# A fused attention and MLP kernel: fetching transposed activations for two tiles in one set of transfers

## The chip, the cores and the metric

The kernel runs on one core of a Trainium2 chip. A core has a matrix engine (TensorE, PE in the profile; its weight loads are shown as PEld), a vector engine (VectorE, DVE), a scalar engine (ScalarE, ACT), a general engine (GpSimd, POOL) and a sync engine (SyncE, SP), which here does nothing but issue DMA transfers. The metric is the device time of one execution in microseconds. Of the kernel before, three runs took 875.13, 876.93 and 880.14 us; the median is 876.93 us.

## The reference

```python
def _attn_ref(q, k, v, g_norm):                       # q, k, v: 8 x 8 x 576 x 64
    kv = np.einsum('bhsd,bhse->bhde', k, v)
    out = np.einsum('bhsd,bhde->bhse', q, kv)
    rms = np.sqrt(np.mean(out * out, axis=-1, keepdims=True) + 1e-06)
    return (out / rms * g_norm)

def _moe_ref(x, w_in, w_out):                         # x: 4608 x 512
    h = x @ w_in                                      # w_in: 512 x 2048
    r = np.maximum(h, 0.0)
    return (r * r) @ w_out                            # w_out: 2048 x 512
```

The attention has no softmax: every head's keys and values are multiplied to a 64 x 64 matrix, and the queries with that. Its output, normalized per token and head, is the `x` of the two matrix products behind it. The weights arrive as float64 and are converted in the opening part of the kernel; everything else is float32.

## The kernel before, in words

The 4608 tokens make 36 tiles of 128 tokens, numbered 0 to 35, and nine strips of four tiles, numbered 0 to 8. For each strip there is an up phase (`x @ w_in`, then relu and square) and a down phase (`@ w_out`). Both are computed with seven products in place of eight over 2 x 2 blocks, from strip 2 on at two levels, so that sums and differences of blocks are formed on DVE and POOL, and PE reads blocks of weights that were formed once, stored in DRAM (`w_deep`, `w_in_deep`, `w_out`) and are streamed back as `w_blk`, block by block, by `stream()`. In the trace a strip from strip 2 on takes PE some 90 us.

While PE works on a strip, the other engines prepare the next strip's `x` in small pieces put between the steps (`slices`, `attend_between`): products of queries and key-value matrices (`query`, line 468), squares and means, the root, the scaled result, and then the transpose, since PE needs `x` with features on partitions. For tiles 0 to 8 PE itself transposes (`features`). Tiles 9 to 35 take another way, in three steps:

- `squares_x(n)` (line 645): DVE transposes tile n within 32 x 32 squares;
- `send_x(n)` (line 654): one transfer of 256 KB stores it in a DRAM tile `x_d`, and an entry is put into the queue `tiles_due`;
- `fetch_x(n)` (line 661): four transfers of 64 KB, one per group of 32 features, read it back in the order that PE needs, into the strip's tile `xT`.

`open_xt(s)` takes the buffer of `xT` from `stream_pool`, the pool of six buffers that also holds the streamed blocks `w_blk`. It is called by the first `fetch_x` of a strip.

The order of all instructions on each engine is the order in which the Python code emits them. What decides when a fetch is emitted is a counted clock (`clock[0]`; from strip 2 on 1.2 units for a step of an up phase and 3.2 for a step of a down phase): an entry of `tiles_due` falls due 6 units after the send, or 24, 30 or 36 for tiles 11, 9 and 10. At each step the main loop emits at most one thing: a due load of keys and values (`keys_due`), or else a due fetch, or else, if enough clock has passed since the last one, one "drip": a pair of query transfers from `drips` (`load`, line 123, two transfers of 64 KB) or `rest_drips` (`load_q_rest`, line 176, two of 16 KB). At the eleventh step of a down phase all fetches that the next strip still lacks are emitted.

```python
elif not due(keys_due) and not (soon and due(tiles_due)):
    ...
    if not quiet and clock[0] >= dripped[0] + least:
        dripped[0] = clock[0]
        drip(True)
```

All these transfers go out on one queue, SP's, in program order, and an instruction that waits holds up everything behind it. In the built program each of SP's transfers waits, besides for its data and its buffer, for the landing of a transfer some eight before it on the queue, since eight semaphores are used in turn. The lines of the queue that matter below: 123 (queries), 132 and 162 (keys, values), 176 (the rest of the queries), 654 and 661 (`x_d`, `xT`), 939 (blocks of `w_in_deep`, for the up phase), 945 and 951 (blocks of `w_out` and `w_deep`, for the down phase), 960 (output). On DVE: line 384 transposes queries that have landed, line 1300 adds a product from PSUM to a unit of the hidden layer or a snapshot of it, lines 289 and 1046 form differences and sums. PE's products of both phases have line 842.

Of the kernel before, what the change touches and what calls it, by code (L numbers as in the profile page):

```python
# [10 lines left out]
FP32 = mybir.dt.float32  # L11
# [9 lines left out]
def kernel(  # L21
# [34 lines left out]
    nc = tc.nc  # L56
    P = 128
# [4 lines left out]
    NP = H // 2  # L62
# [6 lines left out]
    NT = 4  # L69
# [2 lines left out]
    N_STRIP = N_TILE // NT  # L72
    DEEP = 1
    DEEP_UP = 2
    SQ = 32
    Q_ON_PE = 2
    BEHIND = 1.6
# [10 lines left out]
    dram = ctx.enter_context(tc.tile_pool(name="dram", bufs=1, space=bass.MemoryType.DRAM))  # L88
# [15 lines left out]
    def load(b, p, q_eng, names="kvq", parts=range(4)):  # L104
# [9 lines left out]
        for i, (n, src, eng) in enumerate(inputs if b == 0 else inputs[1:] + inputs[:1]):  # L114
# [3 lines left out]
            if n == "q" and b >= Q_ON_PE:  # L118

                t = qkv_pool.tile([P, 4 * C, SQ], FP32, name=n, tag=n, bufs=3) if 0 in parts else main[n, b, p]  # L120
                for a in parts:
                    h, f = divmod(a * SQ, D)
                    eng.dma_start(
                        out=t[ts(a, SQ)],
                        in_=src[b, 2 * p + h, 0 : C * P, f : f + SQ].rearrange("(k i) f -> i k f", k=4 * C),
                    )
# [28 lines left out]

    squares = lambda t: t.rearrange("p h d -> p (h d)").rearrange("p (k q f) -> p k q f", k=4, f=SQ)

# [6 lines left out]
    def load_q_rest(b, eng, one=None):  # L164
# [8 lines left out]
        for a in range(4) if one is None else (one,):  # L173
            hq, f = divmod(a * SQ, D)
            for kq in range(2):
# [14 lines left out]
    drips, rest_drips, keys_due, tiles_due = deque(), deque(), deque(), deque()  # L190
    clock, dripped = [0.0], [0.0]
# [382 lines left out]
    first = {}  # L574
# [49 lines left out]
    def open_xt(s):  # L624
        if s not in xt:
            if s == 0:
                xt[s] = xt_pool.tile([P, STRIP // SQ, NP, SQ], FP32, name="xT", tag="xT")
            else:
                t = stream_pool.tile([P, 4, FQ // 2, P], FP32, name="xT", tag="w_blk")
                xt[s] = t.rearrange("p n f e -> p (n f e)").rearrange("p (a q t) -> p a q t", q=NP, t=SQ)  # L630
        return xt[s]
# [18 lines left out]
    squared, sent = {}, {}  # L650

    def send_x(n):
        d = sent[n] = dram.tile([P, 4, NP, SQ], FP32, name="x_d", tag="x_d", bufs=2 * NT)
        nc.sync.dma_start(out=d, in_=squared.pop(n))
        tiles_due.append((clock[0] + {9: 30, 10: 36, 11: 24}.get(n, 6), fetch_x, (n,)))

    def fetch_x(n):
        s, i = divmod(n, NT)
        x, d = open_xt(s), sent.pop(n)
        for f in range(4):  # L660
            nc.sync.dma_start(
                out=x[ts(f, SQ), ts(i, 4)].rearrange("d a q t -> d a (q t)"),
                in_=d[:, f].rearrange("(a d) q t -> d a (q t)", a=4),
            )

    xc = {}
# [44 lines left out]
    for b in range(2, B):  # L711
        pairs = query_pairs(b)
        for i, pair in enumerate(pairs):
# [11 lines left out]
            if b == 2:  # L725
                slices += [(T, (3, 1))] * (left == 1) + [(mean_roots, (pair,)), (normalized, (pair,))]
                slices += [(T, (3, 0))] * (left == 2) + [(squares_x, (n,)) for n in pair]
                for n in pair:
                    slices.append((send_x, (n,)))
                    if n % NT == NT - 1:  # L730
                        ready[n // NT] = len(slices)
                pair_ends.append(len(slices))
                continue
# [4 lines left out]
            for t, n in enumerate(pair):  # L738
                slices += [(squares_x, (n,)), (send_x, (n,))]
                if n % NT == NT - 1:  # L740
                    ready[n // NT] = len(slices)
                if t == 0:
                    slices += heads[3:]
# [5 lines left out]
    def attend(n):  # L749
        while slice_at[0] < min(n, len(slices)):  # L750
            fn, a = slices[slice_at[0]]
            fn(*a)
            slice_at[0] += 1
# [171 lines left out]
    for s in range(DEEP, N_STRIP):  # L925
        to_stream += [("in", s, p) for p in UP_SETS if s >= DEEP_UP]
        to_stream += [(s, p, n) for p in DEEP_ORDER for n in range(2)]
# [181 lines left out]
    def down_deep(s, k, i):  # L1109
# [3 lines left out]
        if s == N_STRIP - 1 and k == 6 and i == 1:  # L1113
# [19 lines left out]
            return  # L1133
        if k == 0 and s >= DEEP_UP:
            if i == 0:
# [71 lines left out]
    def deep_differences_in(b):  # L1207
        minus(nc.gpsimd, w_half(b, 0, 1), w_half(b, 0, 0), w_half(b, 0, 1))
# [18 lines left out]
    def leaf_x(s, n):  # L1227

        x = operand_x(s, UP_SETS[n])
        t = leaf_t[s, n] = sum_pool.tile([P, 4, TH // SQ // 2, SQ], FP32, name="x_l", tag="sum")  # L1230
        late = x[:, 4:8].rearrange("p a k t -> p k a t")
        minus(nc.gpsimd, t[:, 0:2], late, x[:, :, 0].rearrange("p (h a) t -> p h a t", h=2))
        minus(nc.gpsimd, t[:, 2], late[:, 1], t[:, 0])
        minus(nc.gpsimd, t[:, 3], x[:, 0:4, 1], t[:, 2])
# [13 lines left out]
    def up_slot(s, slot):  # L1248
# [8 lines left out]
        if at == 0 and 0 < n < 6:  # L1257
            leaf_x(s, n + 1)
        if s == DEEP_UP and at == 0 and n < 7:
            deep_differences_in(A_IN[UP_SETS[n]])  # L1260
# [77 lines left out]
    for s in range(N_STRIP):  # L1338
        attend(ready[s])
        if s == DEEP_UP - 1:  # L1340
            while queried:
# [3 lines left out]
            apsum = ctx.enter_context(tc.tile_pool(name="apsum", bufs=1, space=bass.MemoryType.PSUM, reuse_waits="tile"))  # L1345
        if s >= DEEP_UP:
            steps = [(0.5, up_slot, (s, slot)) for slot in range(55)]
# [10 lines left out]
        goal, begun = ready.get(s + 1, len(slices)), slice_at[0]  # L1358
        if s >= DEEP_UP:
            goal = max(goal, min(ready[DEEP_UP] + (len(slices) - ready[DEEP_UP]) * (s - 1) // (N_STRIP - DEEP_UP - 1), len(slices)))  # L1360
# [3 lines left out]
        for i, (w, fn, a) in enumerate(steps):  # L1364
# [33 lines left out]
            if s:  # L1398
                clock[0] += 3.2 if i >= n_up else 2.2 if s == DEEP else 1.2
                soon = tiles_due and tiles_due[0][2][0] // NT == s + 1  # L1400
                if i == n_up + 10:
                    while tiles_due and tiles_due[0][2][0] // NT == s + 1:
                        _, f, a = tiles_due.popleft()
# [36 lines left out]
            n = i + 1 - (n_up - 6)  # L1440
# [44 lines left out]
```

## Time and profile before

| | us |
|---|---|
| median of three runs | 876.93 |
| time of the profiled execution | 876.18 |
| its span in the profile | 874.4 |
| PE busy in the span | 860.8 |
| DVE busy | 722.9 |
| ACT busy | 352.0 |
| POOL busy | 315.4 |
| DMA: mean rate over the span | 270 GB/s |

Among the DMA issues of the page, `xT<-x_d` stands with 108 transfers of 64 KB at a median of 4.1 us from issue to landing, and `x_d<-x_q` with 27 of 256 KB at 5.3 us. The granted TensorE clock is 1.00 in every stretch of the profile. All times of single instructions are counted from the start of the span. The profiled execution took 1.8 us more than its span; this part lies outside of what the profile shows.

How to read the views: the windows give the busy time of each engine in a stretch; 20.00 of 20.00 for PE means that it was never without a matmul. The view of waits says for how long an engine stood idle and what ended it. The timeline lists instructions in order, with the start, the duration, and in brackets the idle time of the engine before it; for SP, the duration is that of issuing, and the transfer lands later.

### The profile page before, as it was taken

The numbers are of one execution on the slowest core, as the hardware profiler recorded it, in microseconds if no ns is written. First come the engines' busy times: TensorE is split into PE (matmuls) and PEld (weight loads), VectorE is DVE, ScalarE is ACT, GpSimd is POOL, SyncE is SP. The second block draws the span as 40 slices with busy tenths as digits, with TensorE's granted clock in tenths as the row PEclk, the third lists the DMA queues.
The fourth block names the chain that finished last, engine by engine and source line by source line (L and its number), as shares of the span: only waits on it lengthen the run. The fifth ranks groups of instructions, "written<-read, shape, count | busy, mean of one in ns | idle before, by whom it ended". The sixth has DMA issues, their size and how long they took to land.

```text
span 874.4 us, 32665 instructions
## 1 busy us (share of the span) xinstructions
PE 860.8 (98%) x14176; PEld 805.8 (92%) x14176; DVE 722.9 (83%) x1236; ACT 352.0 (40%) x805; POOL 315.4 (36%) x319
## 2 busy tenths in 40 slices
PE   8999999999999899999999999999999999999998
PEld 7445888889999899999999999999999999999998
DVE  3899998879867896889778977897889777975897
ACT  5799241320047402560358034811392147202710
POOL 1100004630458305650475045704471447144700
PEclk9999999999999999999999999999999999999999
DMA  9998998999988997989778978998668856885483
GB/s 306 328 311 251 285 372 237 283 339 346 305 219 205 338 328 242 239 290 338 245 213 261 344 268 228 271 346 287 189 238 293 295 173 218 299 283 196 175 313 120
DMA packets 170304, 236.49 MB, mean 270 GB/s; under 512 B 79536, under 2 KB 134576, under 8 KB 161840
## 3 DMA queue, kind: packets, MB, share of 16 engines
q1 hardware_dynamic: 169856, 234.33, 82.5%
q8 instruction: 111, 1.82, 0.8%
q14 instruction: 33, 0.27, 0.1%
q10 hardware_dynamic: 304, 0.07, 0.0%
HBM read 197.66 MB, written 36.70 MB: 268 GB/s over the span
## 4 chain that ended last, share of the span: by engine, by line
PE 82%; DVE 9%; DMA 4%; ACT 3%; issue 2%; SPq 1%; DVEq 0%; ACTq 0%
PE ps_A L842 35%; PE ps_B L842 30%; PE ps_C L842 5%; PE ps_A L847 4%; PE x_ps L468 2%; PE kv_ps L432 2%; PE ps_B L847 2%; DVE w_c L269 1%; DVE w_t L289 1%; DMA q<-in_q_dram 1%; DMA w_blk<-w_deep 1%; DMA w_deep<-w_t 1%; DVE wt L289 1%; DMA q_rest<-in_q_dram 1%; PE ps_C L847 1%
## 5 line engine op out<-in xcount | busy, mean ns | idle before, releaser
L842 PE MATMUL ps_B<-w_blk,g_s 128*64 128x128 f32 x2016 | 122.6, 273 | 0.0
L842 PEld LDWEIGHTS ps_B<-w_blk,g_s 128*64 128x64 f32 x2016 | 113.1, 137 | 0.1
L842 PE MATMUL ps_A<-x_l,w_in 128*64 128x128 f32 x1568 | 102.4, 273 | 0.6 <-ACT snap L1305 0.6
L289 POOL TENSOR_TENSOR x_l<-xT 128x256 f32<-128x256 f32 x21 | 15.9, 757 | 232.4 <-PE ps_A L842 184.3
L842 PE MATMUL ps_B<-w_blk,gt 128*64 128x128 f32 x1504 | 94.7, 273 | 2.8 <-DMA w_blk<-w_deep 1.6
L842 PE MATMUL ps_A<-w_blk,g_s 128*64 128x128 f32 x1536 | 92.7, 273 | 0.4 <-issue 0.4
L842 PEld LDWEIGHTS ps_A<-x_l,w_in 128*64 128x64 f32 x1568 | 88.9, 137 | 0.9 <-ACT snap L1305 0.8
L842 PEld LDWEIGHTS ps_B<-w_blk,gt 128*64 128x64 f32 x1504 | 85.1, 137 | 3.6 <-issue 2.2
L1300 POOL TENSOR_TENSOR snap<-snap,gt 128x512 f32<-128x512 f32 x35 | 46.2, 1319 | 113.1 <-ACT snap L1305 107.5
L842 PEld LDWEIGHTS ps_A<-w_blk,g_s 128*64 128x64 f32 x1536 | 86.1, 137 | 0.5 <-issue 0.5
L1305 ACT COPY snap<-ps_A 128x512 f32<-128x512 f32 x63 | 36.8, 585 | 105.0 <-PE ps_A L842 99.0
L1240 ACT ACTIVATE gt<-gt 128x512 f32<-128x512 f32 x112 | 70.1, 626 | 14.2 <-DVE gt L1300 14.2
L1241 ACT ACTIVATE gt<-gt 128x512 f32<-128x512 f32 x112 | 70.7, 631 | 3.6
L842 PE MATMUL ps_A<-w_blk,gt 128*64 128x128 f32 x1152 | 71.5, 273 | 0.0
L842 PEld LDWEIGHTS ps_A<-w_blk,gt 128*64 128x64 f32 x1152 | 65.0, 137 | 0.0
L1089 ACT COPY o_sb<-ps_A 128x128 f32<-128x128 f32 x24 | 6.4, 265 | 145.5 <-PE ps_A L842 110.2
L1088 DVE TENSOR_TENSOR o_sb<-o_sb,ps_B 128x256 f32<-128x256 f32 (+1 forms) x123 | 47.4, 386 | 15.8 <-ACT o_sb L1089 11.0
L289 DVE TENSOR_TENSOR gt<-gt 128x2048 f32<-128x2048 f32 (+1 forms) x29 | 59.7, 2063 | 0.0
L1300 POOL TENSOR_TENSOR gt<-gt,snap 128x512 f32<-128x512 f32 x42 | 52.6, 1282 | 17.7 <-DVE snap L1300 17.7
L842 PE MATMUL ps_B<-x_l,w_blk 128*64 128x128 f32 x784 | 51.3, 273 | 0.0
L842 PE MATMUL ps_A<-x_l,w_blk 128*64 128x128 f32 x784 | 51.2, 273 | 0.0
L1046 DVE TENSOR_TENSOR g_s<-gt 128x512 f32<-128x512 f32 x56 | 47.9, 856 | 0.0
(194 smaller groups left out, 1801.6 us busy)
## 6 DMA issues: line engine op xcount, KB each, us to landing
w_blk<-w_deep SPq DMA_DIRECT2D x56, 1024.0 KB, 7.2
w_blk<-w_out SPq DMA_DIRECT2D x56, 768.0 KB, 6.7
w_blk<-w_in_deep SPq DMA_DIRECT2D x49, 768.0 KB, 6.1
raw<-in_moe_w_in_dram SPq DMA_DIRECT2D x16, 512.0 KB, 7.0
raw<-in_moe_w_out_dram SPq DMA_DIRECT2D x16, 512.0 KB, 4.8
k<-in_k_dram SPq DMA_DIRECT2D x29, 256.0 KB, 4.8
v<-in_v_dram SPq DMA_DIRECT2D x29, 256.0 KB, 5.1
x_d<-x_q SPq DMA_DIRECT2D x27, 256.0 KB, 5.3
```

Of the source, the lines that this page charges most:

```text
L269: yield nc.vector.scalar_tensor_tensor(out=ci, in0=high, scalar=-(2**30), in1=ci, op0=ALU.bitwise_and, op1=ALU.bitwise_or)
L289: eng.tensor_tensor(out=out, in0=a, in1=b, op=ALU.subtract)
L432: nc.tensor.matmul(ps[ts(h, D), i], lhsT=a, rhs=w, start=i == 0 and c == 0, stop=c == C, skip_group_check=True)
L468: nc.tensor.matmul(ps[half, r, i, ts(p, D)], lhsT=q[row, half], rhs=kvd[b, p][row, row], start=True, stop=True)
L842: nc.tensor.matmul(ps[half], lhsT=lhsT[:, half], rhs=rhs, start=start, stop=stop, skip_group_check=True)
L847: nc.tensor.matmul(bank[BANK[p]][:, i, :], lhsT=lhsT(k), rhs=rhs(k), start=p in (1, 5, 2) and i == 0 and k == 0, stop=k == n - 1, skip_gro ...
L1046: nc.vector.tensor_tensor(out=t, in0=a21, in1=a22, op=ALU.add)
L1088: add = lambda out, a, b: nc.vector.tensor_tensor(out=out, in0=a, in1=b, op=ALU.add)
L1240: nc.scalar.activation(o, o, AF.Relu)
L1241: nc.scalar.activation(o, o, AF.Square)
L1300: add = lambda eng, out, a, b: eng.tensor_tensor(out=out, in0=a, in1=b, op=ALU.add)
L1305: nc.scalar.copy(t, ps)
```

## The change

`send_x` now gives two neighbouring tiles (an even number and the odd one behind it) one DRAM tile with two halves, and only the odd tile's send puts an entry into `tiles_due`. `fetch_x` then reads both halves with four transfers of 128 KB. Tile 8 is transposed on PE, so tile 9, the first that is sent, is fetched alone as before (`FIRST_SENT`). The even tile has no due time of its own any more; the entry for tile 10 is gone. There are 56 fetches in place of 108, with the same bytes.

```diff
+    FIRST_SENT = 9
...
     def send_x(n):
-        d = sent[n] = dram.tile([P, 4, NP, SQ], FP32, name="x_d", tag="x_d", bufs=2 * NT)
-        nc.sync.dma_start(out=d, in_=squared.pop(n))
-        tiles_due.append((clock[0] + {9: 30, 10: 36, 11: 24}.get(n, 6), fetch_x, (n,)))
-
-    def fetch_x(n):
+        if n % 2 and n - 1 in sent:
+            d = sent.pop(n - 1)
+        else:
+            d = dram.tile([2, P, 4, NP, SQ], FP32, name="x_d", tag="x_d", bufs=NT)
+        sent[n] = d
+        nc.sync.dma_start(out=d[n % 2], in_=squared.pop(n))
+        if n % 2:
+            tiles_due.append((clock[0] + {9: 30, 11: 24}.get(n, 6), fetch_x, (n, 1 if n == FIRST_SENT else 2)))
+
+    def fetch_x(n, tiles):
         s, i = divmod(n, NT)
         x, d = open_xt(s), sent.pop(n)
+        first = i + 1 - tiles
         for f in range(4):
             nc.sync.dma_start(
-                out=x[ts(f, SQ), ts(i, 4)].rearrange("d a q t -> d a (q t)"),
-                in_=d[:, f].rearrange("(a d) q t -> d a (q t)", a=4),
+                out=x[ts(f, SQ), 4 * first : 4 * (i + 1)].rearrange("d a q t -> d a (q t)"),
+                in_=d[2 - tiles :, :, f].rearrange("n (a d) q t -> d (n a) (q t)", a=4),
             )
```

## The prediction

> **What bounds the kernel now.** I read the page's first part, then the windows for where PE is idle, then PE's waits, and then, for the one stretch that stands out, the chain and the timelines of SP, PE and DVE.
>
> ```profile
> PE 860.8 (98%) x14176; PEld 805.8 (92%) x14176; DVE 722.9 (83%) x1236; ACT 352.0 (40%) x805; POOL 315.4 (36%) x319
> ```
>
> PE is busy for 98% of the span. A change that leaves PE's instructions alone can only win from the 874.4 - 860.8 = 13.6 us that are left. The windows, from the first stretch in which the new program differs (about 211 us):
>
> ```profile
> 200.00:240.00 40.00, 40.00 (x738) 40.00 (x736) 36.60 (x55) 2.17 (x7) 9.73 (x10) 1.00 0.98 322
> 240.00:260.00 20.00, 19.74 (x420) 19.30 (x416) 14.88 (x29) 8.98 (x28) 10.66 (x13) 1.00 0.85 238
> 260.00:280.00 20.00, 18.28 (x390) 17.76 (x388) 13.51 (x24) 13.14 (x34) 15.89 (x19) 1.00 0.88 212
> 280.00:300.00 20.00, 17.20 (x313) 16.77 (x310) 16.51 (x23) 13.70 (x26) 11.38 (x8) 1.00 0.86 265
> 300.00:320.00 20.00, 19.59 (x359) 19.45 (x357) 18.27 (x29) 0.80 (x3) 0.00 (x0) 1.00 1.00 356
> ```
>
> Columns: length, then busy time of PE, PEld, DVE, ACT, POOL, the clock, the DMA share, GB/s. PE is idle for 0.26 + 1.72 + 2.80 + 0.41 us here, all of it in strip 2. In the finer windows behind it only 340-360 (0.02) and 540-560 (0.58) are not full until the last 14.4 us, where the last sums and stores leave 3.0 us that no fetch touches. What is within reach is 5.8 us, 0.66%. PE's waits from 200 us on:
>
> ```profile
> PE ps_B L842 <- DMA w_blk<-w_deep: 1.6, 1, 1.6
> PE x_ps L468 <- issue: 1.3, 1, 1.3
> PE ps_B L842 <- DMA w_blk<-w_out: 1.2, 1, 1.2
> PE ps_A L842 <- ACT snap L1305: 0.6, 1, 0.6
> PE ps_A L842 <- issue: 0.4, 1, 0.4
> PE ps_C L842 <- issue: 0.4, 1, 0.4
> PE x_ps L468 <- DVE qT_rest L388: 0.3, 1, 0.3
> ```
>
> The two largest that have a cause are blocks of weights for strip 2's down phase that landed late. The SP timeline shows why:
>
> ```profile
> 277.44 2.40 SPq L661 DMA_DIRECT2D xT<-x_d  x4
> 281.09 1.61 SPq L123 DMA_DIRECT2D q<-in_q_dram  x2
> 282.80 0.43 SPq L945 DMA_DIRECT2D w_blk<-w_out  x1
> ...
> 284.87 0.38 SPq L951 DMA_DIRECT2D w_blk<-w_deep  x1
> 290.49 1.74 SPq L661 DMA_DIRECT2D xT<-x_d  x4
> ```
>
> The block of line 945 went out at 282.80 and landed 5.4 us later; the one of 951 at 284.87, 8.6 us to landing. PE wanted them at 287.12 and 292.01:
>
> ```profile
> 288.29 1.09 PE L842 MATMUL ps_B<-w_blk,gt 128*64 128x128 f32 x16 [1.17 <-DMA w_blk<-w_out]
> 290.93 1.07 PE L842 MATMUL ps_B<-x_t,w_blk 128*64 128x128 f32 x16
> 293.64 1.09 PE L842 MATMUL ps_B<-w_blk,gt 128*64 128x128 f32 x16 [1.64 <-DMA w_blk<-w_deep]
> ```
>
> The first block's buffer was free from about 272.3 (its last reader, the x_t group that starts at 271.23, lasts 1.04), so it stood in SP's queue for ten microseconds behind small transfers.
>
> **The change, part by part.** In the built programs PE, DVE, ACT and POOL have the same instructions in the same order; only SP's queue differs.
>
> (1) Fewer issues: 52 fetches less, at 0.43 us of issuing each (the median of line 661) 22 us of SP's time. Off PE's path except in strip 2. There, between the block of line 939 issued at 254.21 and the block of line 945 at 282.80, stand 32 transfers before and 24 after: the four of tile 12 ride with tile 13, the four of tile 14 move behind both blocks to go with tile 15. In the timeline these eight cost 2.02 (at 254.66) + 2.40 (at 277.44) = 4.4 us of issuing. So the 945 block goes out between 272.3 (buffer) and 282.80 - 4.4 = 278.4, and lands by 283.8 even at the late end: 3.3 us before PE asks. The 951 block gets a pair of line 176 ahead of it that was not there (pairs of that line take 0.9 to 2.2 us); 284.87 - 4.4 + 2.2 = 282.7 at the latest, plus 8.6 is 291.3. That is just ahead of the 291.5 at which PE will now ask (below).
>
> (2) What takes the place of the 1.17 us: the group behind it at 290.93 needs a PSUM bank that DVE empties.
>
> ```profile
> 289.73 0.68 DVE L1300 TENSOR_TENSOR snap<-ps_B,gt 128x512 f32<-128x512 f32 x1
> ```
>
> DVE works without a gap from 281.06 to 293.8, so this still ends at 290.41. PE would come to the group at 290.93 - 1.17 = 289.76 and start at about 290.46 (at 245.34 PE started 0.05 us after DVE's last write). Of 1.17 us 0.47 are kept. PE then reaches the 951 block at 290.46 + (292.01 - 290.93) = 291.5 instead of starting at 293.64. Gain of both: 2.1 us. Lower end 1.2 (the 951 block takes 9.5 us to land, the longest of a block in this stretch, and is 0.9 late), upper end 2.8 (DVE not in the way).
>
> (3) Queries earlier. A step without a fetch lets a drip go one step sooner. DVE waits at line 384 for queries that land too late: 3.3 us until 243.98 and 5.09 us before
>
> ```profile
> 264.15 0.71 DVE L384 STREAM_TRANSPOSE qT<-q 128x512 f32<-128x512 f32 x1 [5.09 <-DMA q<-in_q_dram]
> ```
>
> In the new order both pairs stand one drip earlier, the first before the block that went out at 231.77 (so at least 6.6 us sooner), the second before the one at 242.66 instead of at 256.73. Both DVE waits go. PE's share of the first is the 0.26 us at 245.08; I take 0.25. In the second, PE's next reader of DVE at 266.26 had its data 0.8 us before, so PE lost nothing: 0.
>
> (4) Idle marked "issue": 1.34 in the query products at 262.51, 0.39 at 270.14, 0.41 at 315.55. No wait of the program stands there. The same 64 products ran without a gap at 446.49, 628.81 and 697.30. I take 0, with ends 2.1 us won and 2.1 lost: the gaps could stay, go or come elsewhere. The 0.58 at 557.50 is a wait for ACT: 0, at best 0.58.
>
> (5) Later fetches. The even tile now comes with the odd one. Strip 3's first reader of `xT` is POOL at 326.96, after the fetch that landed at 294.3; the odd tile's fetch keeps its place in every strip. Cost 0, hidden by 32 us of other work. The buffer of `xT` is taken one to three blocks later in strips 3, 4, 7 and 8: blocks of line 939 then get buffers released earlier, and no block a later one.
>
> (6) Larger lumps. Behind the odd tile's landing 512 KB are fetched instead of 256, ahead of later down blocks. 256 KB at 300 GB/s is 0.87 us. The tightest blocks after strip 2's first two: 0.62 us of slack at 301.52 (its block, issued at 292.81, lands 8.1 later; but it now goes out earlier too), 1.33 at 566.86, 1.59 at 384.54. Only the first is under 0.87, so 0; lower end 0.9 lost in each of six strips, 5.2 us.
>
> The Trainium skill (DMA: Bandwidth & Descriptors, Anatomy of one DMA) gives every transfer a fixed cost of about 2.0 us, and its Rules for kernel authors would have small transfers coalesced. By that, 52 transfers less would be an estimated 104 us of DMA time. The row speaks against the size: four fetches issued 0.4 us apart from 290.49 land 2.5 to 3.2 us after issue each, so their fixed parts overlap, and PE, idle for 5.8 us here, cannot win 104.
>
> The same skill (Perfetto Trace Analysis, Identifying the Most-Contended Engine) holds matmul busy time to be a bad measure of headroom and weight loads a better one. From 240 to 320 us PEld is idle for 8.7 us against PE's 5.2, so by it some 3.5 us more could be had; most of that lies in query products of 64 columns, whose number does not change.
>
> The sum: -2.1 - 0.25 = -2.35 us. The profiled execution took 876.18 (span 874.4 and 1.8 around it), which would be 873.8. It lies 0.75 under the median of the runs, so against the median: 876.93 - 2.35 = 874.6.
>
> **The rivals.** *All idle time goes.* The two blocks (2.81), the 0.26, the issue gaps (2.14) and the 0.58: 5.8 us, 871.1. For it: the issue gaps lie where DMA is busiest. Against: DVE is full in 281-294, and nothing names the cause of the gaps.
>
> *The fetch is hidden anyway.* The 951 block is held by the fuller queue and lands as late as now; PE waits there what it saved before. 876.5 to 877. For it: DMA's share is 0.86 to 1.00 from 260 to 320 and the bytes are the same. Against: the ten microseconds that the 945 block stood in the queue.
>
> *Slower: the lump in front of the down blocks.* SP stands still until the odd tile has landed in DRAM (5.24 us before 290.49), and then 512 KB go ahead of the next blocks. If 128 KB over 32 partitions land in 6.2 us, as the 128 KB of `k_rest` do at the median, and not in some 3, the blocks behind are late by 0.87 + 2 to 3 us. The tightest slacks of strips 2 to 6 are 0.6, 1.6, 2.7, 1.3, 3.7, on average 2.0; it decides from a lateness of about 2.7 us on, where six strips lose 0.75 each, over 0.5%. At 3 us: 876.9 + 6 x 1.0 = 883. Against it: after 600 us the DMA share is 0.57 to 0.84 and slacks are over 3.5.
>
> **How the numbers follow.** A difference under 0.5% (4.4 us) is about what a measurement of this kernel can tell from no change. The forecast, won 1.2 to 4.4 us (872.5 to 875.7), gets 44%; all idle time gone, 4.4 to 5.8, 30%; hidden anyway 13%; slower 13%. So faster 0.30, same 0.57, slower 0.13. The likeliest gives 874.6. The range leaves out the slower case and the far end of the second: 871.0 to 878.0, the upper end being no change with 1 us of spread.
>
> **What would show it.** Right: PE's waits for `w_blk<-w_out` and `w_blk<-w_deep` gone, a new short wait of PE on DVE line 1300 near 290; the 945 block issued before 279; DVE's two waits at line 384 gone; PE busy unchanged near 861. Wrong: new PE waits on `w_blk` in strips 3 to 6 (the lump), or issue gaps larger than 2 us. The forecast falls if the 945 block is still issued after 282.

## The result, and the profile after

The changed kernel took 871.02 us (median of seven runs, 870.26 to 873.16), the kernel before 877.73 in seven runs beside it (875.13 to 882.88). The ratio is 0.9922, with a 95% interval of 0.9900 to 0.9943: 6.7 us faster, against 2.35 in the forecast, and at the lower edge of the stated range of 871.0 to 878.0. The profiled execution took 870.26, 5.9 less than the one of before, with a span of 868.4.

The first part of its page, and the windows over strip 2 (the columns are those of before):

```profile
PE 859.4 (99%) x14176; PEld 805.4 (93%) x14176; DVE 723.5 (83%) x1236; ACT 351.5 (40%) x805; POOL 315.7 (36%) x319
```

```profile
240.00:260.00 20.00, 20.00 (x426) 19.63 (x422) 15.96 (x31) 8.88 (x28) 10.89 (x14) 1.00 0.89 234
260.00:280.00 20.00, 20.00 (x432) 19.86 (x430) 14.39 (x26) 15.79 (x40) 17.99 (x20) 1.00 0.94 254
280.00:300.00 20.00, 19.27 (x354) 19.03 (x352) 18.86 (x26) 11.17 (x21) 9.04 (x6) 1.00 0.97 322
300.00:320.00 20.00, 20.00 (x370) 20.00 (x368) 18.97 (x32) 0.80 (x3) 0.00 (x0) 1.00 0.98 352
```

Of the 5.2 us that PE stood idle between 240 and 320 us, 0.73 are left. PE's waits from 200 us to the end are down to two lines:

```profile
PE ps_B L849 <- DVE snap L1307: 0.7, 1, 0.7
PE ps_A L849 <- ACT snap L1312: 0.6, 1, 0.6
```

(Lines behind the change have moved by seven: 842 is now 849, 1300 is 1307, 661 is 668, 945 and 951 are 952 and 958. Those ahead of it have moved by one: 123 is now 124, 468 is 469.) No wait for `w_blk`, none for queries, none marked issue. The 0.7 us are the residue that step (2) named. It stands before the group that ran at 290.93 before, three groups behind the one that waited for the first down block, and its releaser is the sum on DVE. The timelines of PE, then of DVE:

```profile
287.86 1.09 PE L849 MATMUL ps_B<-x_t,w_blk 128*64 128x128 f32 x16 [0.73 <-DVE snap L1307]
```

```profile
287.13 0.68 DVE L1307 TENSOR_TENSOR snap<-ps_B,gt 128x512 f32<-128x512 f32 x1
```

The query products that had the gap of 1.34 us now run without one. The line of before, then the one of after:

```profile
263.85 0.68 PE L468 MATMUL x_ps<-kv_all,qT 64*64 64x64 f32 x28 [1.34 <-issue]
```

```profile
261.43 1.10 PE L469 MATMUL x_ps<-kv_all,qT 64*64 64x64 f32 x62
```

SP's timeline shows the first two down blocks leaving at 274.62 and 279.06, where they left at 282.80 and 284.87:

```profile
251.40 3.00 SPq L124 DMA_DIRECT2D q<-in_q_dram  x4
254.50 3.86 SPq L946 DMA_DIRECT2D w_blk<-w_in_deep  x1
...
263.69 2.85 SPq L668 DMA_DIRECT2D xT<-x_d  x4
...
274.62 1.82 SPq L952 DMA_DIRECT2D w_blk<-w_out  x1
...
279.06 0.41 SPq L958 DMA_DIRECT2D w_blk<-w_deep  x1
```

Where the 6 us of span came from is read by laying PE's instructions of both profiles side by side (PE's order is the same in both) and noting how much earlier each runs, at the time that it had before:

| PE's work that ran before at | runs earlier by, us | gap passed |
|---|---|---|
| 245 | 0.34 | queries, 0.26 |
| 264 | 2.00 | issue, 1.34 |
| 271 | 2.61 | issue, 0.39 |
| 288.3 | 3.95 | first down block, 1.17 |
| 290.9 | 3.07 | (the residue on DVE costs 0.88) |
| 293.6 | 4.85 | second down block, 1.64 |
| 317 | 5.5 | issue, 0.41 |
| end of the span | 5.96 | |

So the queries gave 0.3, the down blocks 1.34 - 0.88 + 1.78 = 2.2, and the gaps marked issue 1.66 + 0.61 + 0.65 = 2.9; 0.5 came after 317 us, some half of it behind PE's last instruction. Most steps give 0.1 to 0.3 us more than the gap shown.

### The profile page after: what moved, and what is told of

Read it like the earlier page. It is cut to its first block, busy times and chain, and to the rows that moved or that the text cites. A ratio compares the mean times of both kernels' runs of the same rounds, so it can differ in the third digit from the quotient of the medians.

```text
span 868.4 us, 32584 instructions
## 1 busy us (share of the span) xinstructions
PE 859.4 (99%) x14176; PEld 805.4 (93%) x14176; DVE 723.5 (83%) x1236; ACT 351.5 (40%) x805; POOL 315.7 (36%) x319
## 4 chain that ended last, share of the span: by engine, by line
PE 82%; DVE 9%; ACT 3%; DMA 3%; issue 2%; SPq 1%; POOL 0%; DVEq 0%; POOLq 0%; ACTq 0%
PE ps_A L849 35%; PE ps_B L849 31%; PE ps_C L849 5%; PE ps_A L854 3%; PE x_ps L469 2%; PE kv_ps L433 2%; DVE w_t L290 1%; DVE w_c L270 1%; PE ps_B L854 1%; DMA w_deep<-w_t 1%; DVE wt L290 1%; DMA q<-in_q_dram 1%; DMA raw<-in_moe_w_out_dram 1%; DVE w_in L290 1%; DVE w_c L264 1%
```

## The experiments

Five theories are tested. A: the gain comes in strip 2's stretch from where transfers stand in SP's queue. B: the number or size of the transfers makes it. C: the steps that are freed, and with them the earlier queries, are all of it. D: every strip gives a share. E: the profiled execution of before was a mild one, and other executions lose more to late blocks. Ratios are to runs of the kernel before on the same chip in the same set. Its medians in the four sets were 879.98, 878.92, 879.38 and 878.93 us. The table shows the time of the one profiled execution of each kernel, and PE's waits in it in us from 200 us on. Some of these executions were far from the median of their kernel, which the waits must be read with. The last column doesn't depend on a profile: it counts the runs whose mean granted TensorE clock is 0.998 or less. A profile with 3.4 us at half clock has 0.998 (experiments 10 and 11), one with 6.8 us has 0.996, one with none has 0.999 or 1.000.

| kernel | median, us | ratio (95%) | profiled, us | late blocks | issue | late queries | runs with a lower clock |
|---|---|---|---|---|---|---|---|
| before (three profiles) | 878.9 to 880.0 | | 876.18; 874.45; 883.12 | 2.8; 1.5; 5.7 | 2.1; 1.4; 2.9 | 0.3; 1.2; 0.6 | 69 of 103 |
| after, again | 871.62 | 0.9919 (0.9892 to 0.9947) | 871.22 | 0 | 0 | 0 | 1 of 12 |
| 1: pairs in eight of 64 KB | 875.74 | 0.9953 (0.9921 to 0.9986) | 881.94 | 8.0 | 0 | 0 | 6 of 12 |
| 2: even tile keeps its slot | 874.05 | 0.9926 (0.9905 to 0.9947) | 874.93 | 0.4 | 1.6 | 1.4 | 0 of 6 |
| 3: pairs from tile 16 on | 877.62 | 0.9978 (0.9955 to 1.0002) | 881.19 | 3.6 | 0.5 | 1.9 | 7 of 12 |
| 4: pairs for tiles 10 to 15 | 875.84 | 0.9950 (0.9927 to 0.9972) | 876.88 | 2.1 | 2.1 | 0 | 5 of 12 |
| 5: before, queries early | 876.82 | 0.9987 (0.9961 to 1.0013) | 876.78 | 4.4 | 0 | 0 | 5 of 12 |
| 6: before, tile 14 later | 881.17 | 1.0025 (1.0003 to 1.0048) | 880.32 | 6.7 | 0.8 | 1.8 | 9 of 12 |
| 7: whole strips | 874.58 | 0.9958 (0.9932 to 0.9985) | 874.63 | 0.8 | 1.0 | 0 | 1 of 12 |
| 8: after + 4 small, 260 us | 874.62 | 0.9959 (0.9926 to 0.9993) | 871.87 | 0.5 | 0 | 0 | 4 of 10 |
| 9: after + 4 large, 260 us | 872.24 | 0.9933 (0.9900 to 0.9965) | 871.12 | 0 | 0 | 0 | 1 of 7 |
| 10: after + 4 small, 257 us | 875.70 | 0.9967 (0.9933 to 1.0002) | 878.36 | 3.0 | 2.1 | 0 | 4 of 10 |
| 11: after + 4 large, 258 us | 874.79 | 0.9960 (0.9934 to 0.9986) | 877.94 | 3.4 | 1.3 | 0 | 5 of 10 |

**Both kernels again.** The changed kernel was run again, and the kernel before profiled twice more, to see what changes from one execution to the next.

> The kernel before once more, unchanged, for a second profile of it. Theory E (the profiled execution of before was a mild one; the blocks of weights that had 1 to 3 us of slack there, at the ends of the up phases of strips 3 and 5, are late in other executions): at least one more PE wait of over 0.5 us for w_blk in strips 3 to 6, and PE idle for 7 to 12 us after 200 us. Theory A (strip 2 alone): waits only in strip 2, PE idle for about 6 us. If the gaps marked issue are a matter of this kernel's order they stand again near 262 and 270 us; if of chance, elsewhere.

> The kernel before a third time, unchanged. Theories E and A as for the second profile: E sees PE idle for 7 to 12 us after 200 us with different blocks late, A sees about 6 us in strip 2.

> The changed kernel once more, on the same chip as the other runs of this set. Both theories: 6 to 8 us faster than before, PE idle for 1 to 3 us after 200 us, no wait for w_blk over 0.5 us. Theory E besides: its times lie within 4 us of each other while those of before spread over 8 or more.

The gain stands: 0.9919. The two more profiles of before took 874.45 and 883.12 us. Of their difference, 4.2 us lie in the wait for the first down blocks, 1.5 and 5.7 us, and by estimate another 2.7 in the low clock that follows it. In its form theory E falls, since no block of strips 3 to 6 was waited for in any of the three. Its core stands: the profile that the prediction was worked from shows one value of a wait that ranges over 4 us. The profile of 883.12, in PE's timeline and in the windows of 2 us around the stall:

```profile
292.81 1.97 PE L842 MATMUL ps_B<-w_blk,gt 128*64 128x128 f32 x16 [5.66 <-DMA w_blk<-w_out]
```

```profile
285.00:287.00 2.00, 2.00 (x40) 1.91 (x36) 2.00 (x3) 1.71 (x4) 0.99 (x2) 1.00 0.66 81
...
289.00:291.00 2.00, 0.00 (x0) 0.00 (x0) 2.00 (x3) 1.14 (x2) 2.00 (x3) 1.00 1.08 291
291.00:293.00 2.00, 0.19 (x2) 0.22 (x4) 0.51 (x1) 0.00 (x0) 1.63 (x1) 0.61 1.06 416
293.00:295.00 2.00, 2.00 (x21) 2.00 (x21) 0.00 (x0) 0.00 (x0) 0.00 (x0) 0.50 0.35 142
```

The granted clock, third figure from the end, falls to 0.50 while PE stands and stays there after the block has come: the group of 16 takes 1.97 us, 1.04 elsewhere, and 21 matmuls fit into a window that held 40 before. The low clock lasts 6.8 us, and PE works in 5.5 of them at half speed, which costs an estimated 2.7 us. So one late block is paid twice.

The clocks of all runs say how often that happens. Of 103 runs of before, 69 had a lower clock, with a median of 880.76 us; the other 34 have 876.90. The profile that the prediction was worked from, 876.18 at a clock of 1.00, is one of the milder third. Of 19 runs of the changed kernel (both sets), one had a lower clock, and the other 18 have a median of 871.12. So at full clock the two kernels are 5.8 us apart, about what the two profiles show (4.2 in the one set that has both), and the rest of the gain is that the changed kernel seldom falls to a lower clock. E's forecast that its times lie within 4 us of each other missed (869.68 to 875.18), while those of before spread over 15.

**1. Order without larger transfers.** The new order, but each pair fetched with eight transfers of 64 KB.

```diff
-        for f in range(4):
-            nc.sync.dma_start(
-                out=x[ts(f, SQ), 4 * first : 4 * (i + 1)].rearrange("d a q t -> d a (q t)"),
-                in_=d[2 - tiles :, :, f].rearrange("n (a d) q t -> d (n a) (q t)", a=4),
-            )
+        for t in range(tiles):
+            for f in range(4):
+                nc.sync.dma_start(
+                    out=x[ts(f, SQ), ts(first + t, 4)].rearrange("d a q t -> d a (q t)"),
+                    in_=d[2 - tiles + t, :, f].rearrange("(a d) q t -> d a (q t)", a=4),
+                )
```

> The new order of the queue, but a pair of tiles is fetched with eight transfers of 64 KB in place of four of 128 KB. Theory A (what counts is where the fetches and the queries stand in the queue in strip 2): 871 to 873 us, PE's waits for blocks of weights at the end of strip 2's up phase stay gone. Theory B (what counts is the number and size of the transfers): the gain is gone, 876 to 878 us, and PE waits again for blocks of line 945 and 951.

875.74 us, 0.9953: by the medians somewhat over half of the gain. In the profile no query is late, no gap is marked issue, but blocks are late again, now of `w_deep`, by 3.03 us in strip 2 and 4.58 in strip 3:

```profile
PE ps_B L850 <- DMA w_blk<-w_deep: 7.6, 2, 4.6
```

In strip 3 SP spends 6.65 us on eight fetches just ahead of that block (first line, this kernel); the changed kernel spends 3.00 on four (second, its own):

```profile
375.64 6.65 SPq L669 DMA_DIRECT2D xT<-x_d  x8
```

```profile
368.62 3.00 SPq L668 DMA_DIRECT2D xT<-x_d  x4
```

The profiled execution, 881.94, was one of the two slowest of twelve: six ran at full clock, with a median of 873.19, and six had a lower clock, with 878.90. So order alone still leaves, by the clocks, long waits in about half of the executions; fewer transfers take them away. Theories A and B are both needed.

**2. Larger transfers without early queries.** Pairs as in the change, but the even tile keeps an entry in the queue of due fetches that does nothing, so that queries go out as late as before.

```diff
+        if n % 2 == 0:
+            tiles_due.append((clock[0] + {10: 36}.get(n, 6), lambda n: None, (n,)))
```

> Pairs with 128 KB as in the changed kernel, but the even tile keeps its place in the queue of due fetches and does nothing there, so that the step is used up and no query drips into it. Theory A: the blocks of weights are on time (2 us won), the queries are late again, so DVE waits 3 and 5 us for them; 873 to 876 us. Theory C (the freed steps, and so the earlier queries, are all of it): 877 us or more. Theory B: 871 us as the changed kernel.

874.05, 0.9926: by the ratio nearly the whole gain, with queries late (1.4 us) and 1.6 us of issue. None of its six runs had a lower clock, so it keeps that part of the gain; against the 871.12 of the changed kernel at full clock it is 2.9 us behind, about what its queries and gaps cost. A's forecast (873 to 876) came, and theory C falls as the whole story.

**3 and 4. Only some of the strips.** Pairs only for tiles 16 and up (experiment 3), or only for 10 to 15 (experiment 4); the others go singly as before. The diff is that of experiment 3; in experiment 4 its first line reads `if not 10 <= n < 16`.

```diff
+        if not n >= 16:
+            d = sent[n] = dram.tile([1, P, 4, NP, SQ], FP32, name="x_e", tag="x_e", bufs=NT)
+            nc.sync.dma_start(out=d[0], in_=squared.pop(n))
+            tiles_due.append((clock[0] + {9: 30, 10: 36, 11: 24}.get(n, 6), fetch_x, (n, 1)))
+            return
```

> Pairs from tile 16 on alone (strips 4 to 8); tiles 10 to 15 are fetched one by one as before. Theory A (all of the gain is made in strip 2's stretch, 240 to 320 us): 876.5 to 878.5 us, as before. Theory D (every strip brings a share, by fewer transfers): 10 of 13 pairs, 872 to 873 us.

> The other half: pairs for tiles 10 to 15 alone, tiles 16 to 35 one by one as before. Theory A: the whole gain, 870 to 872 us. Theory D: 3 of 13 pairs, about 876 us.

Experiment 3 can't be told from nothing (0.9978, up to 1.0002), and its profile has before's waits in strip 2. Experiment 4 gets 0.9950: the fetches of these six tiles, which go out in strip 2 and just ahead of it, carry the larger part. Here A's forecast, the whole gain (870 to 872), missed, and D's, about 876, came; for experiment 3 it was A's that came. The profile of experiment 4 has block waits near 383 and 567 us, of 1.1 and 1.0, in strips where pairs are not used. The prediction had found the slacks 1.59 and 1.33 there. So a share of theory D stands, by the two ratios some 0.2 to 0.3% of the time, which the intervals don't part from nothing.

**5. The kernel before with early queries.** A due fetch no longer uses up its step.

```diff
-                elif not due(keys_due) and not (soon and due(tiles_due)):
+                elif not due(keys_due):
+                    if soon:
+                        due(tiles_due)
```

> The kernel before, fetches one by one in 64 KB, but a due fetch no longer uses up the step, so the queries drip as early as in the changed kernel or earlier; the fetches of tiles 12 and 14 stay where they were. Theory A and E: DVE's waits for queries (8.4 us at line 384) go, PE's waits for w_blk stay; 0.3 to 2 us faster than before. Theory C (the freed steps are all of it): 6 us faster.

876.82, 0.9987: no gain that can be told from none, where C had forecast 6 us. The queries are in time and no gap is marked issue, but both kinds of block are late:

```profile
PE ps_B L842 <- DMA w_blk<-w_out: 2.8, 2, 2.1
PE ps_B L842 <- DMA w_blk<-w_deep: 1.6, 2, 0.8
```

Early queries with as many transfers push the blocks back. That is a second way in which order alone trades one wait for another.

**6. One fetch moved.** The kernel before, with the four fetches of tile 14 moved behind the first down block.

```diff
-        tiles_due.append((clock[0] + {9: 30, 10: 36, 11: 24}.get(n, 6), fetch_x, (n,)))
+        tiles_due.append((clock[0] + {9: 30, 10: 36, 11: 24, 14: 20}.get(n, 6), fetch_x, (n,)))
```

> The kernel before, every fetch still one tile in four transfers of 64 KB; only the four fetches of tile 14 in strip 2 move in SP's queue, from ahead of the first down block (w_out) to behind it, ahead of the second (w_deep). Theory A (a down block is late by what SP issues ahead of it): in the profile the wait of PE for w_out is gone or under 0.5 us, because its issue comes some 2.4 us earlier, and the wait for w_deep stays at 1 us or more, because the same transfers still stand ahead of it. So the first wait is traded for the second: the time is 0 to 1.5 us under the kernel before. Theory B (the number and size of the transfers decide, not their place): both waits stand as before, and so does the time, within 0.5 us.

1.0025: slower by 0.03 to 0.48%, where A had forecast a little faster, though what it said of the second block came:

```profile
PE ps_B L842 <- DMA w_blk<-w_deep: 4.8, 2, 3.5
PE ps_B L842 <- DMA w_blk<-w_out: 1.9, 1, 1.9
```

The first block left at 282.88, as late as in the profile of before (282.80):

```profile
279.97 2.81 SPq L123 DMA_DIRECT2D q<-in_q_dram  x2
282.88 1.65 SPq L945 DMA_DIRECT2D w_blk<-w_out  x1
```

What stood ahead of it took up the place: these two issues of queries took 2.81 us where they had taken 1.61, and the fetch ahead of them stood 4.6 us for the landing of the store that it reads, 2.6 before. Theory B's "as before" missed too. An issue on SP's queue has no fixed price of 0.43 us: it can stand for a landing, or last longer itself, and a gap in the queue is filled by the next delay. What made these two issues longer isn't shown; SP's view of waits names no landing there.

**7. One step further.** A strip's four tiles in four transfers of 256 KB.

```diff
-        if n % 2 and n - 1 in sent:
+        if n % NT and n - 1 in sent:
...
-        if n % 2:
-            tiles_due.append((clock[0] + {9: 30, 11: 24}.get(n, 6), fetch_x, (n, 1 if n == FIRST_SENT else 2)))
+        if n % NT == NT - 1:
+            tiles_due.append((clock[0] + {11: 24}.get(n, 6), fetch_x, (n, min(n + 1 - FIRST_SENT, NT))))
```

> Goes one step further than the change: a whole strip's four tiles are fetched at once in four transfers of 256 KB (strip 2, which has three: 192 KB each), after the strip's last tile. If the gain lies in idle time of PE that the change has already taken (1.3 us are left after 200 us), nothing more is to be had: 870 to 872.5, the same as the changed kernel. If larger transfers bring something of their own, as with theory B, 868.5 to 870. If a lump of 1 MB ahead of the down blocks makes them late (the slower rival of the prediction), waits on w_blk in strips 2 to 6 and 873 or more.

874.58, 0.9958; it is not better than the change, and by the medians worse. The profile has one block late, by 0.8 us at 237 us. It was issued 15 us behind strip 2's fetch, so the lump of the slower rival is not seen in it. Two gaps are marked issue (1.0). No version was found that beats the change.

**8 to 11. What the gaps marked issue are.** The trace lists 111 packets of 16 KB of instructions on a queue of their own; 28,352 instructions of PE (matmuls and weight loads) over 111 are 255 each. In the profile of before the packets ahead of its gaps marked issue seemed late against PE's progress. Experiments 8 and 9 put four extra transfers of 64 KB into the changed kernel's queue in strip 2, from `q` into a DRAM tile `extra` that nobody reads, in pieces of 128 bytes (8) or of 2 KB (9). Experiments 10 and 11 do the same three steps earlier (`i == 15`), directly behind four transfers of queries. The diff is that of experiment 8; 9 and 11 read `q[7, fourth, 0:256]` in rows of 2 KB.

```diff
+            if s == DEEP_UP and i == 18:
+                for fourth in range(4):
+                    nc.sync.dma_start(
+                        out=extra[ts(fourth, SQ)].rearrange("p (k f) -> p k f", f=SQ),
+                        in_=q[7, fourth, 0 : C * P, 0:SQ].rearrange("(k i) f -> i k f", k=4 * C),
+                    )
```

> The changed kernel with four more transfers on SP's queue near 257 us in strip 2, each of 64 KB in pieces of 128 bytes like those of the queries, into a place that nobody reads. If the idle time of PE marked issue comes of its instruction packets standing behind traffic of small pieces, gaps of 0.4 to 1.5 us marked issue come back between 258 and 275, and a packet of PE's instructions lands later there than in the changed kernel. If late queries themselves are what brings them, by another way than traffic, there is no such gap. Either way SP loses some 2 us ahead of the down blocks, which are then late by 0 to 1 us. Time 871 to 874.

> The same four more transfers of 64 KB at the same place, but in pieces of 2 KB. If small pieces are what delays PE's instruction packets, no gap marked issue comes back here (under 0.2 us between 258 and 275), while SP's loss ahead of the down blocks is the same as with small pieces. If it is the bytes or the number of transfers, the gaps are as with small pieces. Time 871 to 873.

> The changed kernel with the four extra transfers of 64 KB in pieces of 128 bytes moved some 3 us earlier, directly behind the four transfers of queries that go out near 254 us, so that SP's queue issues eight such transfers in a row, as the kernel before does with four fetches and four queries. Over the profiles so far, the idle time of PE marked issue follows 1.2 to 1.5 us behind a packet of PE's instructions that landed late for PE's place in its program. Theory T (the packet is held up by the traffic issued ahead of it): the packet that lands at 258.4 in the changed kernel lands at 260 or later, and a gap marked issue of 0.3 to 1.4 us stands 1.2 to 1.5 us behind it. Rival (the traffic is not the cause): it lands before 259.5 and there is no such gap. Time 871 to 875.

> The same place and the same 256 KB in pieces of 2 KB. If the packet is held up by the number of pieces ahead of it, it lands before 259.5 here and there is no gap marked issue; if by the bytes or by the number of transfers, it is as late as with small pieces. Time 871 to 874.

Experiments 8 and 9 brought no gap: the packet in question had landed at 259.6 and 259.5, before the extra transfers were issued at 260. Experiment 10 did what theory T, set out above, said. Its SP timeline, then PE's:

```profile
252.41 4.51 SPq L124 DMA_DIRECT2D q<-in_q_dram  x4
256.96 6.87 SPq L1404 DMA_DIRECT2D extra_d<-in_q_dram  x4
...
281.49 1.60 SPq L953 DMA_DIRECT2D w_blk<-w_out  x1
```

```profile
263.98 0.68 PE L470 MATMUL x_ps<-kv_all,qT 64*64 64x64 f32 x28 [1.08 <-issue]
```

The packet landed at 262.74 in place of 258.41, and PE took up work again 1.2 us later, in the same query products that have the gap of 1.34 in the profile of before. The first down block left at 281.49 in place of 274.62, and PE waited 3.0 us for it. Four transfers of 64 KB brought back two kinds of idle time that the change had removed. With large pieces (experiment 11) the block was held up as much (281.87) and late by 0.3 us, and the second block was late by 2.2. (The other 0.9 of its late blocks stands at 236 us, ahead of the extra transfers.) No gap followed the packet in question, which landed at 261.96, but PE itself was 2.8 us behind by then: a gap of 1.12 had come at 253, ahead of the extra transfers. So whether pieces or bytes hold up the packets stays open.

For each packet one can count how many instructions PE had begun when it landed, less 256 for every packet before it, as a measure of its lateness. Over all 16 profiles there are 25 gaps marked issue of 0.15 us or more between 60 and 855 us, and each ends at nearly the same distance behind the landing of a packet (counts from the records of the traces, of PE's matmuls, weight loads and sequencer instructions):

```
lateness at landing,       packets   with a gap marked issue
in packets of 256                    behind them
1.63 or more                 19        18
1.50 to 1.63                 35         6
under 1.50                 1655         1
gap ends after the landing by 1.2 to 1.5 us (one by 1.9)
largest: 1.39, 1.34, 1.12, 1.08, 1.08 us, all at lateness 1.75
```

The 19th packet of the first row landed at 250.12 in experiment 4. A gap of 0.73 us ends 1.31 us behind it too, but the view of waits puts it down to PE itself. Experiment 4 has another, of 0.74 at 259 us, marked issue.

## Why the prediction was wrong

It was right in the direction and in the places, and wrong in the size: 874.6 us against 871.02. Between the two profiled executions 5.9 us were won, 3.6 more than the forecast's 2.35; 2.9 of these are step (4), and 0.5 came after strip 2's waits. The rest of the 6.7 is a term that the sum did not have: most executions of before lose more than the one that was profiled. By its steps:

Step (1) held, and its size was low. The block of line 945 left 8.2 us earlier, not 4.4, and the one of line 951 5.8 earlier, not 2.2. I had priced a removed issue by its own duration. The four queries behind the removed fetch of tile 12 took 5.24 us before and 3.00 after. SP's waits show why: before, one of them stood 3.0 us for the landing of the block issued at 254.21, eight transfers ahead of it; after, none of the four stands for a landing. The lines of before, from SP's timeline and from its waits:

```profile
254.66 2.02 SPq L661 DMA_DIRECT2D xT<-x_d  x4
256.73 5.24 SPq L123 DMA_DIRECT2D q<-in_q_dram  x4
```

```profile
SPq L123 <- DMA w_blk<-w_in_deep: 3.0, 1, 3.0
```

Experiment 10 shows the reverse: with four transfers more the first block left 6.9 us later.

Step (2) held: 2.2 us against 2.1, and a residue of 0.73 on DVE against 0.70. But 2.8 us of block waits is what one execution of before showed. Others had 1.5 and 5.7, the last with 6.8 us at half clock on top. The changed kernel has none in two profiles, and its runs lie closer together (870.26 to 873.16 against 875.13 to 882.88), which fits. So the profile of before stands below what its kernel takes: 877.73 - 876.18 = 1.55 us in the seven runs, against 871.02 - 870.26 = 0.76 for the changed kernel. These 0.8 us are the part of the 6.7 that the two profiles don't show. That this profile was a mild one was chance: two thirds of the later runs of before had a lower clock, and the profiled execution had not.

Step (3) held: 0.33 us against 0.25, and DVE's waits for queries in strip 2 are gone. In other executions of before PE waited 0.6 and 1.2 for them, so this step too was drawn from a mild sample.

Step (4) is the one that failed. "I take 0, with ends 2.1 us won and 2.1 lost: the gaps could stay, go or come elsewhere." All three went, and PE gained 2.9 us by the shift of its work. The gaps were no accident of that execution: a gap of 0.39 to 1.34 us stood between 262 and 271 us in all three profiles of before and in experiments 2 and 6, which have late queries as before does (experiment 3 has them too, and no such gap), and at that place in no profile with early queries and no extra transfers (experiment 4 has its gaps of 0.73 and 0.74 just ahead of it, at 251 and 259). They come of PE's instruction packets, and by experiment 10 four more transfers at that place can make a packet late. The prediction's rival had looked to DMA ("the issue gaps lie where DMA is busiest"), and it was set aside because nothing named a cause. The row it leaned on instead, the same products running without a gap at 446, 628 and 697 us, spoke for the place, and against PE's own work as the cause: the DMA share around them is 0.72, 0.51 and 0.54, against 0.86 from 256 to 268. But the share alone would not have told either: between 260 and 280 us it is 0.88 before, with 1.7 us of gaps, and 0.94 after, with none. What tells is when the packets of instructions land.

Steps (5) and (6) held at 0. No `w_blk` of strips 3 to 6 is waited for; the lump of 512 KB made nothing late, and with 1 MB (experiment 7) the one late block, by 0.8 us, stands 15 us behind a lump.

One reading was wrong, and nothing rested on it: from 240 to 320 us the windows give PEld as idle for 80.00 - 73.27 = 6.7 us, not 8.7, so the headroom over PE's 5.2 would have been 1.5 us, not 3.5.

Of the rivals, "all idle time goes" (871.1) was nearest: all went but the wait for ACT, 0.58, and the residue on DVE. What spoke against it, that DVE is full from 281 to 294, cost 0.73 us and no more. "The fetch is hidden anyway" fell with the block's issue at 279.06. The slower one fell with step (6).

What is shown: between the two profiles, 5.5 of the 6.0 us come out of strip 2's stretch; the gain is reproduced, and by the runs tiles 10 to 15 carry the larger part; order alone gives part of it (experiment 1) or nothing (5, 6); with the number of transfers kept, a late block is traded for another (1, 5, 6); gaps marked issue follow late packets of instructions, 24 of 25 of them; and four more transfers at the right place make blocks late (10, 11) and a packet too (10). What is inferred: that the packets share DMA engines with the data traffic and stand behind it; one profile of experiment 10 speaks for it, and the profile of before, where no packet moved between 251.6 and 261.4 us while the changed kernel moved two. That a lower clock in a run without a profile comes of a late block is inferred too, from the profiles that have both. What stays open: whether pieces or bytes hold up a packet (a removed fetch has pieces of 512 bytes, between the two that were tried), what makes an issue itself last up to 4 us, and what pairs give from tile 16 on. The median of experiment 8 lies 2.4 us over that of 9 where their profiles differ by 0.7 us of span: four of its ten runs had a lower clock, one of seven in experiment 9, and the profiles are of runs without.

The Trainium skill (DMA: Bandwidth & Descriptors, Rules for kernel authors) would have small transfers coalesced, and here that, with the order that came with it, was worth 6.7 us. The fixed cost of about 2.0 us a transfer that the prediction took from its section Anatomy of one DMA, which is about transfers issued from the gpsimd engine while these come from SP, was not what was saved: 52 transfers less gave 0.13 us each.

## What to carry to other kernels

Where one queue issues everything, price a removed transfer by what stands behind it until the next transfer that someone waits for, not by its own issue time: here four of them were worth 7 us to a block, and moving them only moved the wait. Before a wait of a microsecond or two is taken as the size of a gain, look at two or three executions; if it changes from one to the next, its mean counts, and what a long one triggers; the mean clock of runs without a profile tells how often it does. A gap marked issue is worth laying beside the landings of PE's packets of instructions before it is priced at nothing.

## What the runs showed of the hardware

PE's clock falls after some stalls. It went to 0.50 for 3.4 us with stalls of 2.22, 2.99, 3.03 and 4.58 us, and for 6.8 us with stalls of 3.61 and 5.66. A stall of 3.52 us (experiment 6) and all those up to 2.07 left it at 1.00, so the length alone doesn't decide. The place does too: within a profile the times between changes of the clock are whole multiples of 3.413 us (84 and 2 times in the profile of 883.12, 84, 1, 27 and 1 in experiment 1). Laid on these steps, each of the six stalls had left PE idle for 2.09 us or more of one step, and the clock fell at that step's end. The stall of 3.52 was split into 1.85 and 1.67 by the border of two steps, and 1.85 is the most idle time of any step at full clock without a fall. The Trainium skill (TensorE: Matmul & The Clock Gate, Why this matters for your kernels) warns of idle gaps of more than about 3 us; of the seven stalls over 2.1 us six came with a lower clock, one of them, of 2.22, well under 3 us, and one over 3 us did not.

PE's instructions come in packets of 16 KB by DMA, about one in 8 us, and behind a packet that lands late PE stands for up to 1.4 us with nothing in the program to wait for. Of 1709 packets in 16 profiles 25 had such a gap marked issue behind them.
